# Freeing the key tile from VectorE's drain, and cutting wq into 32, 16 and 16 KB rows

## The chip, the cores and the metric

The kernel runs on one core of one Trainium2 chip. The metric is the device time of one execution in microseconds (us). The engines are named as in the profile: PE is TensorE, PEld its weight loads, DVE is VectorE, ACT is ScalarE, POOL is GpSimd, SP is SyncE; a "q" behind a name (SPq, ACTq, PEq) is that engine's instruction queue. L162 is line 162 of the kernel.

## What is computed

One decode step of a parallel block. `x` has 512 numbers, there are 32 query heads on 8 key heads, and each key head has a cache of 65,536 positions of 128 numbers for the keys and as many for the values, all fp32:

```
xn = layernorm(x)
q = (xn @ wq) as 32 heads of 128
o = softmax(q k^T / sqrt(128)) v          # 4 query heads share a key head
y = x + o @ wo + relu(xn @ w1) @ w2
```

The two caches are 537 MB of the 561 MB that the kernel reads from HBM.

## The kernel before

**Tiles.** `kt` and `vt` hold one chunk each of keys and values: 128 partitions x 16,384 fp32, so 64 KB a row and 8.39 MB (megabytes of 10^6 bytes) a chunk. There are 32 chunks of each (8 heads x 4 parts). Both tiles are single: a new chunk of keys can only be loaded when PE has read the old one. `wt` holds w1 and later w2. `kt` is also used for wq ahead of the first keys, and for wo behind the last.

**SP's queue** issues nearly all loads, in a fixed order: three pieces of wq (L151, L159), w1 (L160), then a wait for the semaphore `kfree` and the first keys K0 (L162). Then a loop: wait for `vfree`, load a chunk of values (L165), wait for `kfree`, load the next keys (L167). Behind it come wo (L173), w2 (L177) and the store (L179). ACT's queue issues two small loads of `x` at the start (L234: 128 rows of 16 bytes into `xT`; L235).

**The start.** ACT, PE, DVE and POOL compute the layer norm of `xT`; POOL then waits for the semaphore `ends` (a piece of wq, L213) and copies xn into `qpad` (L214). PE's "turn" 0 multiplies qpad with wq in `kt`; a turn is 8 rounds of 4 matrix products, each round covering 2,048 columns. Turns 1 to 32 are the scores of the 32 chunks, and turn 33 is wo; all run the same lines (L307 to L320). `turn_scores` is DVE's side: it waits for two rounds each time (`p2d`), transposes 1,024 columns out of PSUM (L367), and gives PE a pair of banks back (`free`). In turn 0, two drains (L369) also hold `free` back until a later piece of wq has landed, so that PE doesn't read columns that aren't there: rounds 4 and 5 need `free` to reach 3, rounds 6 and 7 need 4. In turn 0 a DVE nop (L366) gives `kfree` when PE's rounds are done.

**A chunk.** After the four transposes DVE drains (L384), takes the maximum (L385), exchanges it over PE, and updates the running maximum (L386 to L392). ACT waits for that (`bias`), computes the correction `corr` (L254, which gives `kfree`), then the probabilities (L256, which give `v`). PE waits for the values and the probabilities and multiplies them (L292); behind that L299 gives `vfree`.

Of the kernel before, what the change touches and what calls it, by code (L numbers as in the profile page):

```python
# [8 lines left out]
AF = mybir.ActivationFunctionType  # L9
# [3 lines left out]
P = 128  # L13
# [4 lines left out]
GROUP = 4  # L18
# [19 lines left out]
XA = D // P  # L38
WIDE = 4
ROUNDS = 8  # L40
WQ_CUTS = [4096, 4096, 8192]
WQ_SEMS = ["ends", "k", "wq2"]
WO_CUTS = [16, 8, 8]
W2_CUTS = [6, 4, 2, 1, 1]
W2_SUM = 12
# [4 lines left out]
def take(e, sem, n=1):  # L50

    return e.sem_inc(sem, -n).wait_op(sem, n, "sem-ge")  # L52


def starts(cuts):
    return [sum(cuts[:i]) for i in range(len(cuts) + 1)]
# [3 lines left out]
def attention_and_mlp_kernel(  # L60
# [12 lines left out]
    sp, pe, dve, act, pool = nc.sync, nc.tensor, nc.vector, nc.scalar, nc.gpsimd  # L73
    scale = float(DH) ** -0.5

    def sbuf(name, *shape):
        return nc.alloc_sbuf_tensor(name, list(shape), F32).ap()
# [3 lines left out]
    def sem(name):  # L81
        if name not in sems:
            sems[name] = nc.alloc_semaphore(name)
        return sems[name]

    def after(ins, name, n=1):

        return ins.wait_op(sem(name), n, "sem-ge")
# [33 lines left out]
    diff = sbuf("diff", P, GROUP)  # L122
    corr = sbuf("corr", P, 2, GROUP)
# [18 lines left out]
    v_row = v[0].rearrange("(n p b) d -> n p (b d)", p=P, b=NB)  # L142
    wq_at, wo_at, w2_at = starts(WQ_CUTS), starts(WO_CUTS), starts(W2_CUTS)

# [5 lines left out]

    load = sp.dma_start(kt[:, : WQ_CUTS[0]], wq_row[:, : WQ_CUTS[0]]).then_inc(sem(WQ_SEMS[0]), 16)  # L151
    tc.no_tile_sem_insts.add(load.ins.name)
# [3 lines left out]
    inside = section.enter_context(tc.tile_critical(sync_engine=mybir.EngineType.Pool, no_gpsimd_drain=True))  # L156
    for i in range(1, len(WQ_CUTS)):
        cut = slice(wq_at[i], wq_at[i + 1])
        sp.dma_start(kt[:, cut], wq_row[:, cut]).then_inc(sem(WQ_SEMS[i]), 16)  # L159
    sp.dma_start(wt, w1_row).then_inc(sem("w1"), 16)  # L160
# [23 lines left out]
    def link(ins):  # L184

        if chain[0]:
            after(ins, "pool", chain[0])
        chain[0] += 1
        return ins.then_inc(sem("pool"), 1)
# [21 lines left out]
    link(pool.tensor_mul(st[:, 7:8], st[:, 5:6], st[:, 6:7]))  # L211
    link(pool.tensor_scalar_mul(xn, xc, st[:, 7:8]))
    take(pool, sem("ends"), 16)  # L213
    after(pool.tensor_copy(qpad[:, :XA], xn), "pool", chain[0]).then_inc(sem("q"), 1)  # L214
    f = DFF_ALL
    w1_of = [wt[:, a * f : (a + 1) * f] for a in range(XA)]
# [34 lines left out]
    act.preload_act_table(AF.Exp)  # L251
    with act.Fori(0, NCH):
        take(act, sem("bias"))
        act.activation(corr, diff.unsqueeze(1).to_broadcast([P, 2, GROUP]), AF.Exp).then_inc(sem("kfree"), 1)  # L254
        for g in range(GROUP):
            last = act.activation(  # L256
                probs[:, :, g], tr[:, :, g], AF.Exp, bias=nb_new[:, g : g + 1], scale=scale,
                accum_out=part_sum[:, g : g + 1],
            )
        last.then_inc(sem("v"), 1)  # L260
# [101 lines left out]
    def turn_scores(gates=(), free=None):  # L362

        for s in range(ROUNDS // 2):
            if free and s == ROUNDS // 2 - 1:
                after(dve.nop(), "p2d", s + 1).then_inc(sem(free), 1)  # L366
            ins = after(dve.transpose(tr2[:, s * 1024 : (s + 1) * 1024], pair[s % 2]), "p2d", s + 1)  # L367
            if s < len(gates):
                ins = after(dve.drain(), gates[s], 16)  # L369
            ins.then_inc(sem("free"), 1)  # L370
# [1 line left out]
    dve.memset(ones, 1.0)  # L372
    dve.memset(banks, 0.0).then_inc(sem("zero"), 1)
    after(dve.reciprocal(st[:, 5:6], st[:, 4:5]), "ln", 3).then_inc(sem("ln"), 1)
    turn_scores(["wq2", "wq2"], free="kfree")
    dve.drain()
    dve.tensor_reduce(qall, of_own_row(NQ, XA), axis=AX.X, op=ALU.add).then_inc(sem("dve"), 1)
    take(dve, sem("p2d"), 4)
# [1 line left out]
    with dve.Fori(0, HEADS) as h:  # L380
        dve.tensor_copy(qpad[:, :GROUP], qall[:, bass.ds(h * GROUP, GROUP)]).then_inc(sem("q"), PARTS)
        with dve.Fori(0, PARTS):
            turn_scores()
            dve.drain()  # L384
            dve.reduce_max(m, tr.rearrange("p b i -> p i b")[:, :GROUP, :], axis=AX.X).then_inc(sem("d2p"), 1)  # L385
            after(dve.reduce_max(mg, pma[:GROUP, :P], axis=AX.X), "p2d", 5).then_inc(sem("dve"), 1)  # L386
            after(
                dve.tensor_scalar(dg, ident[:GROUP, :GROUP], mg, -scale, op0=ALU.mult, op1=ALU.mult), "dve", 1  # L388
            ).then_inc(sem("d2p"), 1)
            after(dve.tensor_tensor(nb_new, pmb[:, :GROUP], nb_run, op=ALU.min), "p2d", 6).then_inc(sem("dve"), 1)  # L390
            after(dve.tensor_sub(diff, nb_new, nb_run), "dve", 2).then_inc(sem("dve"), 1)
            after(dve.tensor_copy(nb_run, nb_new), "dve", 3).then_inc(sem("bias"), 1)  # L392
            after(dve.tensor_copy(o_sb.rearrange("p b d -> p (b d)"), acc), "p2d", 7).then_inc(sem("d2p"), 1)  # L393
            dve.tensor_mul(lo_run, lo_run, corr).then_inc(sem("dve"), 1)
            take(dve, sem("p2d"), 8)
            after(dve.tensor_add(lo_run, lo_run, lo_new), "dve", 4).then_inc(sem("dve"), 1)  # L396
            take(dve, sem("dve"), 5)
        dve.reciprocal(diff, lo_run[:, 0, :]).then_inc(sem("dve"), 1)
        dve.memset(nb_run, 3.0e38)
        after(  # L400
            dve.tensor_mul(oT[:, bass.ds(h * GROUP, GROUP)], lo_run[:, 1, :], diff), "dve"
        ).then_inc(sem("dve"), 1)
        take(dve, sem("dve"), 2)
# [53 lines left out]
```

## Time and profile before

| | us |
|---|---|
| median of 3 runs | 1303.04 |
| lowest and highest of them | 1302.91, 1303.61 |
| the profiled execution's own time | 1303.17 |
| its span, first to last instruction | 1301.4 |

So 1.8 us of the profiled execution lie outside the span. The profiled execution shows PE busy 59% of the span, PEld 18%, DVE 21%, ACT 6%, POOL 3%. Starts are counted from the span's start. A landing is the time from a transfer's issue until its semaphore is complete; idle times in brackets stand before an instruction, with what ended them.

### The profile page before, as it was taken

Reading aid. Unit: us, or ns where it says so; the run is one execution under the profiler, and the core shown is the slowest. Engines: PE = TensorE matmul, PEld = TensorE weight load, DVE = VectorE, ACT = ScalarE, POOL = GpSimd, SP = SyncE. Lnnn points to the kernel's source line nnn. Section 1 sums busy time; section 2 is a strip of 40 time slices with the busy share of each in tenths; the row PEclk is TensorE's granted clock in tenths of the full one; section 3 lists DMA queues with packets and bytes.
Section 4 is the critical chain, followed back from the end, with each engine's and each line's share of the span. In section 5 each row is a group of like instructions: output and inputs, shape, how many; then the busy total and the mean of one; then the engine's idle time right before and its main releaser. Section 6 shows DMA issues by size and latency. Waiting matters only on the chain.

```text
span 1301.4 us, 13055 instructions
## 1 busy us (share of the span) xinstructions
PE 771.8 (59%) x5474; PEld 230.8 (18%) x5474; DVE 274.8 (21%) x466; ACT 76.9 (6%) x299; POOL 34.8 (3%) x30
## 2 busy tenths in 40 slices
PE   3365666565665655575566566466566556656667
PEld 1111111111111111121111121111111111112112
DVE  2211222210222221122221122221122221122222
ACT  1000000000000000000000000000000000000000
POOL 1900000000000000000000000000000000000000
PEclk9667877777777777777777787777787776678678
DMA  9999999999999999999999999999999999999998
GB/s 403 451 419 451 419 445 425 441 429 421 449 419 451 419 451 419 443 427 425 445 419 451 419 451 419 445 425 439 431 423 447 419 451 419 447 423 445 425 424 366
DMA packets 11236, 561.02 MB, mean 431 GB/s; under 512 B 1505, under 2 KB 1505, under 8 KB 1890
## 3 DMA queue, kind: packets, MB, share of 16 engines
q1 hardware_dynamic: 11088, 561.00, 99.7%
q10 hardware_dynamic: 146, 0.00, 0.0%
q8 instruction: 1, 0.02, 0.0%
q14 instruction: 1, 0.01, 0.0%
HBM read 560.99 MB, written 0.00 MB: 431 GB/s over the span
## 4 chain that ended last, share of the span: by engine, by line
issue 94%; DMA 3%; POOL 2%; SPq 0%; PE 0%; DVE 0%; POOLq 0%
DMA wt<-w 3%; POOL wt L219 1%; POOL wt L222 0%; POOL wt L224 0%; POOL wt L223 0%; SPq L177 0%; SPq L159 0%; PE banks L345 0%; DVE ysb L418 0%; SPq L151 0%; POOL hT L226 0%; SPq L453 0%; POOLq L156 0%
## 5 line engine op out<-in xcount | busy, mean ns | idle before, releaser
L313 PE MATMUL banks<-kt,qpad 128*32 128x512 f32 x2176 | 311.1, 735 | 308.6 <-PEq L52 306.9
L292 PE MATMUL banks<-vt,probs 128*16 128x512 f32 x2048 | 270.4, 688 | 87.5 <-PEq L52 87.5
L367 DVE STREAM_TRANSPOSE tr<-banks 128x1024 f32<-128x1024 f32 x136 | 170.0, 1250 | 469.9 <-PE banks L313 466.1
L313 PEld LDWEIGHTS banks<-kt,qpad 128*32 128x32 f32 x2176 | 84.4, 132 | 508.2 <-issue 496.2
L292 PEld LDWEIGHTS banks<-vt,probs 128*16 128x16 f32 x2048 | 68.8, 107 | 302.4 <-issue 302.4
L281 PE MATMUL banks<-wt,ones 128*1 128x448 f32 x768 | 118.8, 771 | 0.0
L393 DVE COPY o_sb<-banks 128x512 f32<-128x512 f32 x32 | 22.1, 692 | 457.2 <-PE banks L292 457.2
L254 ACT ACTIVATE corr<-diff 128x8 f32<-128x8 f32 x32 | 6.7, 209 | 1180.1 <-ACTq L52 1180.1
L256 ACT ACTIVATE probs<-tr,nb_new 128x128 f32<-128x128 f32 x128 | 65.9, 522 | 0.0
L276 PE MATMUL banks<-ident,m 128*4 128x128 f32 x32 | 9.8, 306 | 78.9 <-DVE m L385 78.9
L302 PE MATMUL banks<-sel,o_sb 128*128 128x4 f32 x256 | 32.8, 252 | 18.7 <-PEq L52 18.7
L302 PEld LDWEIGHTS banks<-sel,o_sb 128*128 128x128 f32 x256 | 31.0, 191 | 20.6 <-issue 20.6
L226 POOL TENSOR_SCALAR hT<-ysum 128x14 f32<-128x14 f32 x1 | 0.3, 256 | 1218.6 <-DVE ysum L405 1218.6
L385 DVE TENSOR_REDUCE m<-tr 128x4 f32<-128x512 f32 x32 | 32.2, 1005 | 2.9
L281 PEld LDWEIGHTS banks<-wt,ones 128*1 128x1 f32 x768 | 20.1, 99 | 56.5 <-issue 55.9
L277 PE MATMUL banks<-dg,ones 4*128 4x4 f32 x64 | 14.8, 299 | 20.0 <-DVE dg L388 20.0
L256 ACT ACTIVATION_READ_ACCUMULATOR probs<-tr,nb_new 128x1 f32 x128 | 23.9, 187 | 0.0
L276 PEld LDWEIGHTS banks<-ident,m 128*4 128x4 f32 x32 | 2.6, 81 | 108.0 <-DVE m L385 108.0
L219 POOL TENSOR_SCALAR wt<-wt,xn 128x1792 f32<-128x1792 f32 x4 | 19.1, 4797 | 16.4 <-DMA wt<-w 16.4
L277 PEld LDWEIGHTS banks<-dg,ones 4*128 4x128 f32 x64 | 12.0, 233 | 27.2 <-DVE dg L388 27.2
L299 PEld LDWEIGHTS banks<-part_sum,ones 128*128 128x128 f32 x64 | 9.5, 188 | 27.2 <-issue 27.2
L396 DVE TENSOR_TENSOR lo_run<-lo_run,banks 128x8 f32<-128x8 f32 x32 | 5.2, 163 | 40.0 <-DVEq L52 40.0
(69 smaller groups left out, 91.1 us busy)
## 6 DMA issues: line engine op xcount, KB each, us to landing
kt<-wq SPq DMA_DIRECT2D x2, 2048.0 KB, 9.5
kt<-wq SPq DMA_DIRECT2D x1, 4096.0 KB, 21.0
kt<-wo SPq DMA_DIRECT2D x1, 4096.0 KB, 14.5
kt<-wo SPq DMA_DIRECT2D x2, 2048.0 KB, 21.2
wt<-w SPq DMA_DIRECT2D x1, 3584.0 KB, 29.0
wt<-w SPq DMA_DIRECT2D x1, 1536.0 KB, 11.7
wt<-w SPq DMA_DIRECT2D x1, 1024.0 KB, 13.8
kt<-k SPq DMA_DIRECT2D x32, 24.6
```

The lines of the kernel that those rows point to most:

```text
L219: last = pool.tensor_scalar_mul(w1_of[a], w1_of[a], xn[:, a : a + 1])
L256: last = act.activation(probs[:, :, g], tr[:, :, g], AF.Exp, bias=nb_new[:, g : g + 1], scale=scale, accum_out=part_sum[:, g : g + 1],)
L276: after(pe.transpose(pma[:GROUP, :P], m, ident), "d2p").then_inc(sem("p2d"), 1)
L277: after(pe.matmul(pmb[:, :GROUP], ones[:GROUP, :], dg, start=True, stop=True), "d2p", 2).then_inc(sem("p2d"), 1)
L281: ins = pe.matmul(hrow[32 * c : 32 * c + 1, :], ones[:, :1], hb[:, :, 32 * c : 32 * c + 32], start=True, stop=True,)
L292: last = pe.matmul(acc[c : c + WIDE * GROUP, :], probs[:, b : b + WIDE, :].rearrange("p b g -> p (b g)"), vt[:, b * DH : (b + WIDE) * DH], ...
L299: pe.matmul(lo_new[:, 0, :], ones, part_sum, start=True, stop=True).then_inc(sem("vfree"), 1)
L302: last = pe.matmul(lo_new[:, 1, :], o_sb[:, b, :], sel[:, b, :], start=(b == 0), stop=(b == WIDE - 1),)
L313: last = pe.matmul(pair[s // 2 % 2][32 * c : 32 * c + 32, s % 2 * 512 : s % 2 * 512 + 512], qpad, kb[:, s * 16 : s * 16 + 16, c, :], start ...
L367: ins = after(dve.transpose(tr2[:, s * 1024 : (s + 1) * 1024], pair[s % 2]), "p2d", s + 1)
L385: dve.reduce_max(m, tr.rearrange("p b i -> p i b")[:, :GROUP, :], axis=AX.X).then_inc(sem("d2p"), 1)
L393: after(dve.tensor_copy(o_sb.rearrange("p b d -> p (b d)"), acc), "p2d", 7).then_inc(sem("d2p"), 1)
```

## The change

Two things are edited. The pieces of wq are 8,192, 4,096 and 4,096 columns (rows of 32, 16 and 16 KB), not 4,096, 4,096 and 8,192. The first piece signals `ends`, the second a semaphore `wq1` of its own, the third `wq2`. POOL, which waits for `ends`, raises `k` for PE's turn 0 (the second piece did that before), and DVE's two drains of turn 0 wait for `wq1` and `wq2`, not both for `wq2`. And in each chunk `kfree` comes from DVE's drain behind the four transposes (L384), not from ACT's `corr` (L254).

```diff
-WQ_CUTS = [4096, 4096, 8192]
-WQ_SEMS = ["ends", "k", "wq2"]
+WQ_CUTS = [8192, 4096, 4096]
+WQ_SEMS = ["ends", "wq1", "wq2"]
...
     take(pool, sem("ends"), 16)
+    pool.sem_inc(sem("k"), 16)
     after(pool.tensor_copy(qpad[:, :XA], xn), "pool", chain[0]).then_inc(sem("q"), 1)
...
-        act.activation(corr, diff.unsqueeze(1).to_broadcast([P, 2, GROUP]), AF.Exp).then_inc(sem("kfree"), 1)
+        act.activation(corr, diff.unsqueeze(1).to_broadcast([P, 2, GROUP]), AF.Exp)
...
-    turn_scores(["wq2", "wq2"], free="kfree")
+    turn_scores(["wq1", "wq2"], free="kfree")
...
             turn_scores()
-            dve.drain()
+            dve.drain().then_inc(sem("kfree"), 1)
```

## Rows read from the trace of the kernel before

**Rows 1.** The page: DMA busy tenths in 40 slices, SP's queue, HBM traffic.

```profile
DMA  9999999999999999999999999999999999999998
q1 hardware_dynamic: 11088, 561.00, 99.7%
HBM read 560.99 MB, written 0.00 MB: 431 GB/s over the span
```

**Rows 2.** Windows: first to last key wait in the loop; engines, PEclk, DMA share, GB/s.

```profile
64.38:1265.12 1200.74, 723.84 (x5115) 216.40 (x5111) 249.30 (x431) 69.85 (x280) 0.00 (x0) 0.75 1.00 433
```

**Rows 3.** Timeline of PE: start, length, what; score and value products after their loads.

```profile
50.95 8.51 PE L313 MATMUL banks<-kt,qpad 128*32 128x512 f32 x64 [24.48 <-PEq L52]
...
495.86 9.61 PE L292 MATMUL banks<-vt,probs 128*16 128x512 f32 x64 [4.19 <-PEq L52]
515.21 8.49 PE L313 MATMUL banks<-kt,qpad 128*32 128x512 f32 x64 [7.81 <-PEq L52]
534.56 8.76 PE L292 MATMUL banks<-vt,probs 128*16 128x512 f32 x64 [3.44 <-PEq L52]
...
1250.65 9.40 PE L313 MATMUL banks<-kt,qpad 128*32 128x512 f32 x64 [8.59 <-PEq L52]
```

**Rows 4.** Timeline of one chunk, from its last transpose, and of a later chunk.

```profile
485.63 1.25 DVE L367 STREAM_TRANSPOSE tr<-banks 128x1024 f32<-128x1024 f32 x1 [0.47 <-PE banks L313]
...
490.03 0.21 ACT L254 ACTIVATE corr<-diff 128x8 f32<-128x8 f32 x1 [35.53 <-ACTq L52]
...
490.47 0.33 SPq L167 DMA_DIRECT2D kt<-k  x1
...
506.03 0.33 SPq L165 DMA_DIRECT2D vt<-v  x1
...
1227.03 0.33 SPq L167 DMA_DIRECT2D kt<-k  x1
...
1231.29 8.83 PE L292 MATMUL banks<-vt,probs 128*16 128x512 f32 x64 [0.84 <-PEq L52]
```

**Rows 5.** Timeline of the end: wo is issued, the last values' product starts.

```profile
1265.12 1.29 SPq L173 DMA_DIRECT2D kt<-wo  x3
...
1270.01 7.06 PE L292 MATMUL banks<-vt,probs 128*16 128x512 f32 x64 [1.32 <-PEq L52]
```

**Rows 6.** Timeline of the start.

```profile
0.73 0.39 SPq L151 DMA_DIRECT2D kt<-wq  x1
0.97 0.39 ACTq L234 DMA_DIRECT2D xT<-x  x1
...
1.34 0.83 SPq L159 DMA_DIRECT2D kt<-wq  x2
2.22 0.64 SPq L160 DMA_DIRECT2D wt<-w  x1
...
9.48 0.20 ACT L240 ACTIVATE xc<-xT 128x4 f32<-128x4 f32 x1 [6.23 <-DMA xT<-x]
...
15.21 5.88 PE L313 MATMUL banks<-kt,qpad 128*32 128x512 f32 x32 [3.03 <-PEq L52]
...
22.83 3.64 PE L313 MATMUL banks<-kt,qpad 128*32 128x512 f32 x32 [1.75 <-DVEq L369]
...
26.66 0.33 SPq L162 DMA_DIRECT2D kt<-k  x1
```

**Rows 7.** DMA issues of the start, one stretch each, then the store: KB, us to landing.

```profile
kt<-wq SPq DMA_DIRECT2D x1, 2048.0 KB, 7.4
xT<-x ACTq DMA_DIRECT2D x1, 2.0 KB, 8.4
kt<-wq SPq DMA_DIRECT2D x1, 2048.0 KB, 11.7
wt<-w SPq DMA_DIRECT2D x1, 3584.0 KB, 29.0
kt<-k SPq DMA_DIRECT2D x1, 23.9
y<-ysb SPq DMA_DIRECT2D x1, 2.0 KB, 1.4
```

## The prediction, made before the changed kernel ran

> **What bounds the kernel now.** I read the page first, to see which engine is full. None is, but the transfers are: every slice of the DMA line is full, and SP's one queue keeps the 16 DMA engines 99.7% busy for 561 MB [rows 1]. The next question is whether the queue ever runs dry between two chunks, because that is where an earlier release of the keys' tile could pay. The view of windows says no: over the 1200.74 us from the first wait for keys to the last one the DMA share is 1.00 at 433 GB/s [rows 2]. A share is an average, so I went to the timeline of PE and took the starts of the products that wait for a load. Values at 495.86, keys at 515.21, values at 534.56: steps of 19.35 us for 8.39 MB, which is 433 GB/s [rows 3]. From keys K0 (50.95) to keys K31 (1250.65) there are 62 steps in 1199.70 us, which is 19.350 each [rows 3]. The mean over 62 equals the single step to 0.01 us, so all dry spells together are at most 62 x 0.01 = 0.6 us. The kernel is one unbroken stream of rows, with a lead-in ahead of it and a tail behind it. Nothing can win but a shorter stream, lead-in or tail, and anything can lose that leaves the queue empty for a moment.
>
> **Part 1: `kfree` from DVE's drain.** In the chunk shown the last transpose ends at 485.63 + 1.25 = 486.88. `corr` starts at 490.03 and ends at 490.24; SP issues the next keys at 490.47, so 0.23 us behind it [rows 4]. After the change SP should issue at about 486.9 + 0.2 = 487.1, some 3.4 us earlier, in 32 chunks. The naive gain is 32 x 3.4 = 109 us. I cost it at nothing, because the transfer of the values covers it: the values that were issued before those keys land at 495.86, 5.4 us after the issue at 490.47 [rows 3, 4]; the shortest such cover I found among the 32 chunks is 1231.29 - 1227.03 = 4.3 us [rows 4]. An issued load needs far less than that to be ready: the 2 KB store from the otherwise idle queue lands 1.4 us after its issue [rows 7]. So the keys' rows already stand in the queue when the values' last rows go, and standing there 3.4 us longer moves nothing. Without that cover the price would be its lack, chunk by chunk. The next issue behind the keys on SP is that of the next values (506.03 in the row, waiting for `vfree`); it doesn't move, because the values' product that frees `vt` still starts when the values land, and it has 515.21 - 506.03 = 9.2 us of cover [rows 3, 4]. wo is released by the same drain: it is issued at 1265.12 now, 4.9 us ahead of the landing of the last values, and will be about 3 us earlier, with the same result [rows 5].
>
> The drain stands on DVE anyway and now also raises a semaphore; ACT's `corr` no longer does. The trace has no drain with a semaphore by itself. Below, its cost is nothing; above, I take 0.2 us, the whole hand-over that was just seen from `corr` to SP, ahead of the maximum in each chunk. 0.2 us late probabilities would delay PE only where the values had landed already; PE still sits idle 0.84 us for the values in the chunk at 1231.29 and several us in others [rows 3, 4]. So nothing, at both ends.
>
> [...]
>
> **Part 2: the pieces of wq.** Bytes, number of transfers and number of rows are the same (three pieces of 128 rows), so the stream is not shorter. What moves is who waits for what in the first 31 us.
>
> *The gates.* Now PE starts turn 0 at 15.21, stops after 5.88 us, is idle 1.75 us until DVE's drain has seen the last piece, and runs 3.64 us more; SP issues K0 0.19 us behind it, at 26.66 [rows 6]. The new gates let PE run on with the third quarter of wq, so up to 1.75 us of that stall goes. It would only bring K0's issue forward, and that is covered: w1, issued at 2.22, lands at 2.22 + 29.0 = 31.2, 4.6 us later, and K0's landing at 26.66 + 23.9 = 50.6 is one step of 19.35 behind that [rows 6, 7]. So: no gain.
>
> *The long rows.* This is what I think is less obvious. `xT`, 2 KB in 128 tiny rows on ACT's queue, lands 8.4 us after its issue, while the store of the same size and shape lands after 1.4 us [rows 7]. So about 7 us of it is waiting among wq's rows on the same 16 engines. The first piece lands at 0.73 + 7.4 = 8.1, the second at 1.34 + 11.7 = 13.0: 4.9 us for 2 MB, in eight 16 KB rows on each engine, so 0.61 us a row [rows 6, 7]. `xT` lands at 0.97 + 8.4 = 9.4, 1.24 us behind the first piece, which is two rows: it got through as the tenth row of each engine passed. If it goes by rows, ten rows after the change are the eight 32 KB rows of the new first piece, which lands where the old first two did, at 13.0, and two 16 KB rows: 13.0 + 1.2 = 14.3. So `xT` comes 4.9 us later. The bounds are no delay (if it didn't go by rows) and 7.0 us (if the whole wait doubled with the row). I take 4.9, since the wait ends two rows behind a piece.
>
> The layer norm and turn 0 hang on `xT`: 15.21 - 9.48 = 5.7 us from ACT's first instruction to PE's start [rows 6]. The new gate of POOL on `ends` isn't later than that (13.0 against a layer norm that ends near 20). So PE starts turn 0 at 15.21 + 4.9 = 20.1. The last piece lands where it did (just ahead of 22.83), so the drains don't hold PE: the first comes behind two of eight rounds, a quarter of the turn's 9.5 us, and a transpose of 1.25 us [rows 4], at 23.7 or later. So turn 0 takes 5.88 + 3.64 = 9.52 us (score turns took 8.49 to 9.40 [rows 3]), and K0 is issued at 20.1 + 9.5 + 0.2 = 29.8, or at 28.8 with the shortest turn. That is 3.1 us later than now.
>
> *The cover of K0.* The queue's last rows before K0 are w1's, which land at 31.2. K0 must be issued ahead of that by what an issue takes besides its own rows: 1.4 us by the store, 7.4 - 4.9 = 2.5 us by the first piece of wq [rows 7]. So the latest harmless issue lies between 28.8 and 29.9. Against 29.8 the queue is dry for 0 to 1.0 us; I take the middle, 0.45 us. V0 is issued right behind K0 and has 19 us of cover. A dry spell here is not given back, since the stream behind it has no slack.
>
> [...]
>
> **The sum.** Against the profiled execution: 1303.17 + 0 (32 earlier issues) + 0 (gates) + 0.45 (start) = 1303.6. The runs' median is 0.13 below the profiled execution, so 1303.5 for a median. A measurement of this kernel tells apart about 0.2%, 2.6 us; the forecast is no change by that measure.
>
> **The rivals.** *The rows don't matter* (12%): `xT` waits for something else than rows in number, K0 is issued at about 24.9, and the change does nothing: 1303.0. For it: no row shows the order of single rows. Against it: 8.4 us against 1.4. *The wait doubles* (5%), the rival on the slower side: `xT` comes 7.0 us later, PE starts at 22.2, K0 is issued at 31.9, the queue is dry for 2.0 to 3.1 us, and the time is 1305.0 to 1306.1. It decides from a K0 issue at about 31.4 to 32.5 (the latest harmless one plus 2.6 us). Against it: only the first piece's rows get longer, the rows behind it stay at 16 KB. *Hidden gaps* (3%): the 3.4 us in each chunk do buy something, because keys that stand in the queue earlier let each engine run through more evenly; even 0.07 us a step would be 4.5 us, 1298.6. Against it: 62 steps that equal one another. The forecast, a start that costs 0 to 1.0 us, has the remaining 80%.
>
> **Range and chances.** Forecast and first rival span 1303.0 to 1304.0 on the median's scale; with the runs' own spread (-0.1 to +0.6) and about half of the way to the doubled wait, 1302.3 to 1305.0. Faster than 1300.4 needs the hidden gaps: 3%. Slower than 1305.6 needs the upper half of the doubled wait, or a late K0 for another reason: 5%. The same: 92%.
>
> **What would show it.** Right: SP's keys issue some 0.2 us behind the fourth transpose's end, with steps still at 19.35 us; `xT` landing about 13.3 us after its issue; PE's turn 0 starting near 20 with no idle time in its middle; K0 issued near 29.8; K0's scores starting at 51.0 to 52.0, not 50.95. Wrong: a step shorter than 19.3 us, an `xT` that lands at 9.4, or scores of K0 later than 53.

## The result

The changed kernel takes 1305.14 us (median of 22 runs, 1304.13 to 1306.69), the kernel before 1303.26 us (22 runs, 1302.84 to 1304.18). The ratio is 1.0015, with a 95% interval of 1.0009 to 1.0021: 1.9 us slower, too little for the 0.2% that the prediction took as measurable, yet clear of zero. The forecast was 1303.5 us in a range of 1302.3 to 1305.0; the measured median lies 0.14 us above the upper end of that range. The profiled execution took 1305.65 us, with a span of 1303.9 us.

In the changed kernel the lines behind L213 have numbers that are one higher. The page still shows one full stream of loads (compare [rows 1]):

```profile
DMA  9999999999999999999999999999999999999998
q1 hardware_dynamic: 11088, 561.00, 99.6%
```

In the loop, from the first wait for keys to the last one, the view of windows shows the same rate as in [rows 2]:

```profile
63.83:1262.88 1199.05, 723.03 (x5115) 216.32 (x5115) 249.06 (x431) 69.14 (x279) 0.00 (x0) 0.75 1.00 433
```

The timeline of one chunk (it answers to [rows 3, 4]) has the last transpose, the next keys' issue, `corr`, and the two products that wait for a load. (The rows count two records for each matrix product, so x64 is the whole of a turn's 32.)

```profile
487.02 1.25 DVE L368 STREAM_TRANSPOSE tr<-banks 128x1024 f32<-128x1024 f32 x1 [0.47 <-PE banks L314]
...
488.55 0.33 SPq L167 DMA_DIRECT2D kt<-k  x1
...
491.46 0.21 ACT L255 ACTIVATE corr<-diff 128x8 f32<-128x8 f32 x1 [35.84 <-ACTq L52]
...
497.88 8.76 PE L293 MATMUL banks<-vt,probs 128*16 128x512 f32 x64 [3.36 <-PEq L52]
...
517.23 9.55 PE L314 MATMUL banks<-kt,qpad 128*32 128x512 f32 x64 [8.67 <-PEq L52]
```

SP issues the keys 0.28 us behind the last transpose (488.27) and 2.9 us ahead of `corr`; under the old release it would have been 0.23 us behind `corr`'s end, at 491.9, so the release came 3.35 us earlier. The step from values to keys is 19.35 us, as before. All that gain is hidden.

The start is where the two traces part (it answers to [rows 6, 7]). First the timeline, then the issues with their us to landing:

```profile
13.56 0.20 ACT L241 ACTIVATE xc<-xT 128x4 f32<-128x4 f32 x1 [10.31 <-DMA xT<-x]
...
19.29 9.34 PE L314 MATMUL banks<-kt,qpad 128*32 128x512 f32 x64 [3.02 <-PEq L52]
...
28.83 0.33 SPq L162 DMA_DIRECT2D kt<-k  x1
...
52.35 9.88 PE L314 MATMUL banks<-kt,qpad 128*32 128x512 f32 x64 [23.71 <-PEq L52]
```

```profile
xT<-x ACTq DMA_DIRECT2D x1, 2.0 KB, 12.5
wt<-w SPq DMA_DIRECT2D x1, 3584.0 KB, 28.9
kt<-k SPq DMA_DIRECT2D x1, 23.1
```

`xT` lands 12.5 us after its issue, not 8.4; everything behind it moves by 4.08 us (13.56 against 9.48 on ACT, 19.29 against 15.21 on PE). Turn 0 runs without its stall, K0 is issued at 28.83 instead of 26.66, and its scores start 1.40 us late (52.35 against 50.95). K0 lands at 28.83 + 23.1 = 51.9, while w1, the load ahead of it, landed at 2.22 + 28.9 = 31.1: 20.8 us, where a step is 19.35. So K0 landed 1.4 to 1.5 us too late.

A load raises its semaphore 16 times and has landed with the last of them; the traces of both kernels have the 16 times of each piece of wq and of each chunk. In the kernel before, K0's sixteen come from 50.12 to 50.61 us, the middle one at 50.26; here they come from 50.44 to 51.91, the middle one at 50.95. So K0 isn't late as one piece: its first part comes 0.3 us later than there, the middle 0.7, the last 1.3. The parts don't catch up with one another: those of the next keys, K1, come from 89.12 to 90.69 (before: 88.82 to 89.31).

In this profile two more pieces came on top. The last values' product starts at 1272.03, which is 2.02 us behind 1270.01 [rows 5], so 0.6 us more were lost in loads behind K0 (V1 to K4, by their landings, though they were issued 7.9 to 11.9 us ahead of the landing of the load before them); and that product took 9.31 us, not 7.06:

```profile
1272.03 9.31 PE L293 MATMUL banks<-vt,probs 128*16 128x512 f32 x64 [3.36 <-PEq L52]
...
1301.27 0.34 SPq L179 DMA_DIRECT2D y<-ysb  x1
```

The windows over that product give PE's granted clock (the column behind POOL): 1.00 in the kernel before, and a mean of 0.75 in the changed one. PE had been idle 1.32 us ahead of the product in the one [rows 5], 3.36 us in the other.

```profile
1270.01:1277.10 7.09, 7.09 (x65) 2.05 (x65) 0.00 (x0) 0.00 (x0) 0.00 (x0) 1.00 1.00 430
```

```profile
1272.03:1281.30 9.27, 9.27 (x65) 2.19 (x65) 0.00 (x0) 0.00 (x0) 0.00 (x0) 0.75 0.98 421
```

Behind it the slowed products of PE, not the last load of w2, ended the chain. The views of the chain that ended last show it, the kernel before first:

```profile
1283.19 14.95 DMA wt<-w
```

```profile
1285.04 9.68 PE banks L314 x64
```

From the start of the last values' product to the end of the span it is 1303.9 - 1272.03 = 31.9 us, against 1301.4 - 1270.01 = 31.4 us. Only 0.16 us of these 0.5 lie ahead of the store's issue (1301.27 - 1272.03 = 29.24, against 29.08); the rest lies behind it.

### The profile page after: what moved, and what is told of

Same layout as the page of the kernel before. It is cut to its first block, busy times and chain, and to the rows that moved or that the text cites. A ratio compares the mean times of both kernels' runs of the same rounds, so it can differ in the third digit from the quotient of the medians.

```text
span 1303.9 us, 13056 instructions
## 1 busy us (share of the span) xinstructions
PE 772.9 (59%) x5474; PEld 231.1 (18%) x5474; DVE 274.7 (21%) x466; ACT 76.0 (6%) x299; POOL 34.8 (3%) x30
## 5 line engine op out<-in xcount | busy, mean ns | idle before, releaser
L293 PE MATMUL banks<-vt,probs 128*16 128x512 f32 x2048 | 267.2, 681 | 81.3 <-PEq L52 81.3
L282 PE MATMUL banks<-wt,ones 128*1 128x448 f32 x768 | 122.2, 791 | 0.0
## 6 DMA issues: line engine op xcount, KB each, us to landing
wt<-w SPq DMA_DIRECT2D x1, 3584.0 KB, 28.9
```

Of the source, the lines that this page charges most:

```text
L282: ins = pe.matmul(hrow[32 * c : 32 * c + 1, :], ones[:, :1], hb[:, :, 32 * c : 32 * c + 32], start=True, stop=True,)
L293: last = pe.matmul(acc[c : c + WIDE * GROUP, :], probs[:, b : b + WIDE, :].rearrange("p b g -> p (b g)"), vt[:, b * DH : (b + WIDE) * DH], ...
```

## The experiments

The theory from here on is A: all is lost at the start, because K0 is issued too late behind w1. The rivals: the earlier release in each chunk disturbs the stream (B), or the long rows cost something of their own (C).

**Each part alone.** The pieces of wq alone, which is the changed kernel with ACT's release as before:

```diff
-        act.activation(corr, ..., AF.Exp)
+        act.activation(corr, ..., AF.Exp).then_inc(sem("kfree"), 1)
...
-            dve.drain().then_inc(sem("kfree"), 1)
+            dve.drain()
```

> The new pieces of wq alone; ACT gives the keys' tile free as before. Theory A (the start: 32 KB rows hold xT back, K0 is issued too late behind w1): all of the loss is here, K0 issued near 28.8 us, its scores near 52.3 instead of 50.95, time 1304.7 to 1305.4. Theory B (the earlier release in each chunk disturbs the stream): no loss here beyond 0.4 us, 1303.0 to 1303.7.

Measured: 1305.63 us against 1303.06 (ratio 1.0024, 1.0013 to 1.0035; its runs spread from 1303.54 to 1313.02). The timeline of its start:

```profile
28.90 0.33 SPq L162 DMA_DIRECT2D kt<-k  x1
...
52.26 8.29 PE L314 MATMUL banks<-kt,qpad 128*32 128x512 f32 x48 [23.54 <-PEq L52]
```

The release by the drain alone, in the kernel before:

```diff
-        act.activation(corr, ..., AF.Exp).then_inc(sem("kfree"), 1)
+        act.activation(corr, ..., AF.Exp)
...
-            dve.drain()
+            dve.drain().then_inc(sem("kfree"), 1)
```

> The release of the keys' tile by the drain alone; wq in 16, 16 and 32 KB rows as before. Theory A: K0 issued at 26.7, its scores at 50.95, the next keys issued 3.4 us earlier in each chunk, steps of 19.35 us, time within 0.4 us of the kernel before (1303.3). Theory B: slower by 0.5 to 1.9 us, with steps longer than 19.35 us in the first chunks.

Measured: 1303.05 us against 1303.06 (ratio 0.9999, 0.9990 to 1.0008). K0 and its scores:

```profile
26.46 0.33 SPq L162 DMA_DIRECT2D kt<-k  x1
...
50.74 8.50 PE L313 MATMUL banks<-kt,qpad 128*32 128x512 f32 x64 [24.48 <-PEq L52]
```

B falls: 32 releases, each over 3 us earlier (3.35 to 3.66 us in the changed kernel's trace), cost nothing and gain nothing. The loss belongs to the pieces of wq. (The ratios in this document compare the means of the runs, so the few long ones above pull at them.)

**Take the long rows away.** The changed kernel with wq in four pieces of 16 KB rows:

```diff
-WQ_CUTS = [8192, 4096, 4096]
-WQ_SEMS = ["ends", "wq1", "wq2"]
+WQ_CUTS = [4096, 4096, 4096, 4096]
+WQ_SEMS = ["ends", "k", "wq1", "wq2"]
...
-    pool.sem_inc(sem("k"), 16)
```

> The changed kernel, but wq in four pieces of 16 KB rows (the gates in their new order, the drain's release kept). Theory A: xT lands at 9.4 us, PE starts turn 0 at 15.2, K0 is issued near 24.9, and the loss is gone: within 0.4 us of the kernel before (1303.3). Theory B: still 0.5 to 1.9 us slower. If the gates' order itself costs something, it shows here too.

Measured: 1304.67 us against 1303.06 (ratio 1.0012, 1.0003 to 1.0021). By its time this speaks against A. The trace tells two things apart. The start is healed, and so is every load up to the last values (1270.03 against 1270.01). Turn 0 starts at 15.13 and K0 is out 1.6 us earlier than in the kernel before, which gains nothing, as its scores start at 50.98:

```profile
15.13 6.87 PE L313 MATMUL banks<-kt,qpad 128*32 128x512 f32 x48 [3.03 <-PEq L52]
...
25.05 0.33 SPq L162 DMA_DIRECT2D kt<-k  x1
...
50.98 9.43 PE L313 MATMUL banks<-kt,qpad 128*32 128x512 f32 x64 [26.11 <-PEq L52]
```

But the store, issued at 1299.13 (before: 1299.09), lands 3.1 us later instead of 1.4 [rows 7]:

```profile
y<-ysb SPq DMA_DIRECT2D x1, 2.0 KB, 3.1
```

So the 1.6 us of this kernel are at its very end, where the changed kernel's store landed after 1.5 us. The same kernel was loaded and measured once more:

> The kernel with four pieces of 16 KB once more, loaded anew. In its first profile all loads land as in the kernel before, yet it is 1.6 us slower, because the store's 16 completions came 3.1 us after its issue instead of 1.4. If that was a matter of where the program or its output lay in that load, it is gone: 1303.0 to 1303.5. If it belongs to the kernel, 1304.5 to 1305 again.

1304.59 us against 1303.21 (ratio 1.0009, 1.0000 to 1.0018), with the store landing after 3.0 us and the loads on time: it belongs to the kernel. It has one load more than the kernel before and the changed one, hence this test, the kernel before with 2 KB loaded for nothing:

```diff
     sp.dma_start(wt, w1_row).then_inc(sem("w1"), 16)
+    sp.dma_start(spare, x.rearrange("(p a) -> p a", p=P)).then_inc(sem("spare"), 16)
```

> The kernel before with one more load, 2 KB that nobody uses, behind w1. If one load more is what makes the store's completions late (1.6 us in the kernel with four pieces and in the one with a quarter of V0 ahead, which both have one load more): the store lands 3.1 us after its issue and the time is 1304.5 to 1305. If not: 1303.0 to 1303.5.

1305.28 us against 1303.24 (ratio 1.0016, 1.0007 to 1.0025). Its loads are 0.3 to 0.5 us late, and the store:

```profile
y<-ysb SPq DMA_DIRECT2D x1, 2.0 KB, 2.8
```

One load more costs some 1.4 to 1.7 us at the store, in all three kernels here that have it (the third is the one with a quarter of V0 ahead, below), and in none of those with the old number. Why, these runs don't show. For the changed kernel, which has the old number, it plays no part.

**Leave the long rows, but get xT through.** The changed kernel, with `xT` issued by SP ahead of wq:

```diff
+    first = sp.dma_start(xT, x.rearrange("(p a) -> p a", p=P)).then_inc(sem("x"), 16)
     load = sp.dma_start(kt[:, : WQ_CUTS[0]], ...)
...
-    act.dma_start(xT, x.rearrange("(p a) -> p a", p=P)).then_inc(sem("x"), 16)
```

> The changed kernel with its 32 KB rows, but SP issues xT ahead of wq in its own queue. Theory A: xT lands within 3 us, wq starts 0.6 us later because its issue stands behind, K0 is issued near 25 (set by the last piece of wq), and no dry spell: 1303.3 to 1303.9, slower than before by at most those 0.6 us. Theory B: 1303.8 to 1305.8.

Measured: 1304.09 us against 1303.06 (ratio 1.0007, 0.9998 to 1.0016), undecided by its interval. `xT` landed 1.8 us after its issue, and the timeline shows K0 issued as early as in the kernel before, though not near 25 as I expected:

```profile
1.18 0.42 SPq L154 DMA_DIRECT2D kt<-wq  x1
...
26.62 0.33 SPq L165 DMA_DIRECT2D kt<-k  x1
...
51.52 8.74 PE L316 MATMUL banks<-kt,qpad 128*32 128x512 f32 x64 [25.07 <-PEq L52]
```

Its scores are 0.57 us late, and 0.45 us of that is wq's own issue, at 1.18 instead of 0.73. w1 lands at 2.67 + 29.1 = 31.8, K0 at 26.62 + 24.5 = 51.1, one step of 19.35 later, so no time is lost between them. The other half of the 1.0 us in the median isn't in its profile. So this run is consistent with A and doesn't prove it.

**Delay K0 and change nothing else.** In the kernel before, 1, 2 or 4 transposes of 1.25 us on DVE stand ahead of the release of K0 (into `vt`, which is still empty):

```diff
-                after(dve.nop(), "p2d", s + 1).then_inc(sem(free), 1)
+                after(dve.nop(), "p2d", s + 1)
+                for i in range(2):
+                    late = dve.transpose(vt[:, i * 1024 : (i + 1) * 1024], pair[1])
+                late.then_inc(sem(free), 1)
```

> The kernel before, with one extra transpose of 1.25 us on DVE (into the still empty vt) ahead of the release of K0 in turn 0, so that K0 is issued near 28.0 instead of 26.66. Theory A (a load that is issued late behind w1 costs 3.75 us besides its rows, as K0 did in the changed kernel, so it must be out by 27.5): 0.5 us slower, 1303.8. The prediction's own sizes (harmless up to 28.8 to 29.9): no loss, 1303.3.

> The same with two extra transposes: K0 near 29.3. Theory A with 3.75 us: 1.8 us slower, 1305.1. The prediction's sizes: 0 to 0.5 us slower, 1303.3 to 1303.8.

> The same with four extra transposes: K0 near 32.0, when the queue is empty. Theory A with 3.75 us: 4.5 us slower, 1307.8. The prediction's sizes: 2.1 to 3.2 us slower, 1305.4 to 1306.5.

Measured against 1303.64 us: 1303.61 (ratio 1.0000, 0.9991 to 1.0009), 1304.76 (1.0016, 1.0007 to 1.0025) and 1305.85 us (1.0018, 1.0009 to 1.0027). The timelines of K0's issue and scores, with one, two and four transposes; behind them, in the same order, K0's lines among the issues with the us to landing:

```profile
27.86 0.33 SPq L162 DMA_DIRECT2D kt<-k  x1
...
51.50 9.01 PE L313 MATMUL banks<-kt,qpad 128*32 128x512 f32 x60 [25.06 <-PEq L52]
```

```profile
28.92 0.33 SPq L162 DMA_DIRECT2D kt<-k  x1
...
51.56 8.97 PE L313 MATMUL banks<-kt,qpad 128*32 128x512 f32 x56 [25.19 <-PEq L52]
```

```profile
31.10 0.33 SPq L162 DMA_DIRECT2D kt<-k  x1
...
53.21 7.37 PE L313 MATMUL banks<-kt,qpad 128*32 128x512 f32 x52 [26.92 <-PEq L52]
```

```profile
kt<-k SPq DMA_DIRECT2D x1, 23.2
```

```profile
kt<-k SPq DMA_DIRECT2D x1, 22.3
```

```profile
kt<-k SPq DMA_DIRECT2D x1, 21.8
```

The second has K0 at the same time as the changed kernel (28.92 against 28.83), with wq and `xT` as before. Its ratio is about the same, 1.0016 against 1.0015, but three of its 11 runs, at 1307.6 to 1307.8 us, make that; its median moved by 1.1 us, that of the changed kernel by 1.9. So a late K0 alone is enough for a loss, and by the medians for more than half of this one. Theory A's own size is not borne out: K0's 23.1 - 19.35 = 3.75 us besides its rows in the changed kernel, taken as a fixed need of any late issue, asked for 0.5, 1.8 and 4.5 us and got 0.0, 1.1 and 2.2.

**The changed kernel once more**, loaded anew:

> The changed kernel once more, loaded anew, for a second profile. If the start's loss belongs to it, K0's scores start 1.3 to 1.5 us later than in the kernel before again; whether the further 0.6 us that its first profile lost in the loads of V1 to K4 and the 0.5 us at the end come back is open.

1304.92 us against 1303.21 (ratio 1.0011, 1.0002 to 1.0020). Its profile:

```profile
28.83 0.33 SPq L162 DMA_DIRECT2D kt<-k  x1
...
52.03 8.35 PE L314 MATMUL banks<-kt,qpad 128*32 128x512 f32 x64 [23.39 <-PEq L52]
...
1270.90 7.06 PE L293 MATMUL banks<-vt,probs 128*16 128x512 f32 x64 [1.34 <-PEq L52]
```

K0's scores are 1.08 us late again; the last values are 0.89 us late, so nothing was lost in between, and the last product ran in 7.06 us. So the two further pieces of the first profile come and go. This profiled execution took 1303.95 us, the second fastest of its 11 runs; what the median run lost beyond it, 1.0 us, stands in no profile.

**Give K0 cover.** The changed kernel with part of V0 issued ahead of the wait for K0, so that the queue lasts longer. First a quarter of V0:

```diff
+    sp.dma_start(vt[:, :V0], v_row[0][:, :V0]).then_inc(sem("v0"), 16)    # V0 = 4096
     take(sp, sem("kfree"))
     sp.dma_start(kt, k[0, 0]).then_inc(sem("k"), 16)
+    take(sp, sem("vfree"))
+    sp.dma_start(vt[:, V0:], v_row[0][:, V0:]).then_inc(sem("v"), 16)
...
+    act.wait_ge(sem("v0"), 16)
     with act.Fori(0, NCH):
```

> The changed kernel with its 32 KB rows and its late xT, but SP issues the first quarter of V0 (4,096 columns, 2.1 MB) behind w1 and ahead of the wait for K0; the rest of V0 follows K0. Theory A (the whole loss of the stream is K0 being issued too late behind w1): K0 is still issued near 28.8 but has some 4.8 us more cover, so the values V1 and all later loads land as in the kernel before, and the time is within 0.4 us of it, but for what the end adds (up to 0.5 us, as in the changed kernel's profile). Rival C (the longer rows or their late xT cost something else): 1.4 to 2 us slower, as the changed kernel.

1305.83 us against 1303.21 (ratio 1.0015, 1.0006 to 1.0024): a miss, for two reasons that its trace shows. It has one load more, and its store lands after 3.1 us. And K0, which lands 4.9 us later behind a quarter of V0 (28.18 + 27.3 = 55.5 against 50.6), now makes K1 late: K1 is issued at 66.43, 3.5 us ahead of the landing of V0's rest (28.62 + 41.3 = 69.9), lands 24.2 us later, and its scores start 1.34 us late (89.44 before). The timeline, then K1's line among the issues:

```profile
66.43 0.33 SPq L168 DMA_DIRECT2D kt<-k  x1
...
90.78 2.79 PE L321 MATMUL banks<-kt,qpad 128*32 128x512 f32 x12 [9.88 <-PEq L53]
```

```profile
kt<-k SPq DMA_DIRECT2D x1, 24.2
```

So an eighth, and wq in two pieces to keep the number of loads:

```diff
-WQ_CUTS = [8192, 4096, 4096]
-WQ_SEMS = ["ends", "wq1", "wq2"]
+WQ_CUTS = [8192, 8192]
+WQ_SEMS = ["ends", "wq2"]
...
-    turn_scores(["wq1", "wq2"], free="kfree")
+    turn_scores(["wq2", "wq2"], free="kfree")
...
-V0 = 4096
+V0 = 2048
```

> The changed kernel with its 32 KB first piece and its late xT, but with cover for K0: the first 2,048 columns of V0 (1.05 MB, 2.4 us) are issued behind w1, ahead of the wait for K0. wq comes in two pieces of 32 KB rows, so that the number of loads stays the same. Theory A (an issue has to lead the end of the queue by some 4 us; K0's 2.35 us in the changed kernel and K1's 3.5 us with a quarter of V0 ahead were too short): K0 leads by 4.8 us or more, K1 by 5 to 6, all values and keys from V0 on land as in the kernel before to 0.1 us, although xT is as late as in the changed kernel; time 1303.0 to 1303.6 if the store completes in 1.4 us. Rival C (the long rows or the late xT cost something by themselves): loads 1 to 1.4 us late.

1303.30 us against 1303.24 (ratio 1.0000, 0.9991 to 1.0009). `xT` and K0 are even later than in the changed kernel, K0 landed 23.0 us after its issue, one step behind the eighth of V0 (2.22 + 31.6 = 33.8), and from K1 on all loads stand 0.13 to 0.16 us behind those of the kernel before:

```profile
14.41 0.20 ACT L247 ACTIVATE xc<-xT 128x4 f32<-128x4 f32 x1 [11.16 <-DMA xT<-x]
...
30.13 0.33 SPq L164 DMA_DIRECT2D kt<-k  x1
...
53.60 8.44 PE L321 MATMUL banks<-kt,qpad 128*32 128x512 f32 x64 [23.66 <-PEq L53]
...
89.60 9.21 PE L321 MATMUL banks<-kt,qpad 128*32 128x512 f32 x64 [10.39 <-PEq L53]
```

Among the issues, the eighth of V0 and K0:

```profile
vt<-v SPq DMA_DIRECT2D x1, 1024.0 KB, 31.6
kt<-k SPq DMA_DIRECT2D x1, 23.0
```

With the long rows, the late `xT` and the early release all in place, cover for K0 gives back the whole loss. That settles A against C: the rows and the late `xT` cost nothing by themselves once K0 has cover. No kernel here beats the kernel before; this one, the release alone and the one with a single transpose equal it.

## Why the prediction was wrong

**What bounds the kernel, part 1 and the gates: right.** The steps stayed at 19.35 us, the keys' issue moved 3.35 us (3.4 forecast) and bought nothing, and the release alone measures 0.9999. No run shows the 0.07 us a step by which the rival of the hidden gaps was sized: with the release alone the 62 steps from K0's scores to K31's take 1199.69 us (50.74 to 1250.43), so 19.35 each. The stall in turn 0 went and gained nothing (with 16 KB rows K0 was even out 1.6 us earlier, and its scores started at 50.98).

**The long rows: the mechanism right, the size off.** `xT` goes by rows, and the packets in the trace say so: its 16-byte rows start in groups of 16, in the changed kernel from 4.75, 5.98, 7.20, 8.41, 9.63, 10.84 and 12.06 us, one group per 32 KB row; with the 16 KB rows of the kernel before the groups lie 0.61 us apart. The eighth group goes 0.01 us behind the seventh, and the 4-byte packets with which this queue's load ends start 0.61 us behind it, at 12.68, so `xT` waited for one 16 KB row behind the first piece, not two: it came 4.08 us later, 4.9 forecast. Turn 0 took 9.34 us, not 9.5. So K0 was issued at 28.83, not 29.8. It was out a microsecond earlier than I feared, and still did more harm: this error hid part of the next one.

**The cover of K0: this is the step that failed.** I took what an issue needs besides its own rows from loads into an empty queue, 1.4 to 2.5 us. With K0 at 28.83 these bounds give a loss of at most 28.83 + 2.5 - 31.2 = 0.1 us. Measured were 1.1 to 1.5 us, and K0's scores started at 52.35 and 52.03, beyond the 51.0 to 52.0 that I had named. The runs allow a table: the lead is how far ahead of the landing of the load in front of it a load was issued; "late" is its landing less that landing less a step of 19.35 (landings are given to 0.1 us).

| load | issued | load ahead lands | lead | late |
|---|---|---|---|---|
| K0, kernel before | 26.66 | 31.2 | 4.6 | 0.0 |
| K0, an eighth of V0 ahead | 30.13 | 33.8 | 3.7 | 0.0 |
| K1, a quarter of V0 ahead | 66.43 | 69.9 | 3.5 | 1.4 |
| K0, one transpose | 27.86 | 31.2 | 3.4 | 0.5 |
| K0, changed kernel | 28.83 | 31.1 | 2.3 | 1.5 |
| K0, changed, loaded anew | 28.83 | 31.2 | 2.4 | 1.1 |
| K0, pieces alone | 28.90 | 31.1 | 2.2 | 1.3 |
| K0, two transposes | 28.92 | 31.1 | 2.2 | 0.7 |
| K0, four transposes | 31.10 | 31.0 | -0.1 | 2.5 |

In this table a lead of 3.7 us or more lost nothing and one of 2.2 to 3.5 us lost 0.5 to 1.5 us, one profile to a row, so the border between them is not sharp: with the pieces alone K1 was issued some 3.8 us ahead (an estimate: V0 landed at 29.62 + 41.5 = 71.1, and PE's second product for the maximum, which starts 1.55 us ahead of K1's issue in the kernel before, started at 65.62 and took 0.2 us longer), yet its scores started at 90.85, 0.2 us more than a step behind V0's product at 71.30. With the queue already empty the loss is 2.5 us, the old upper bound; what I had not thought of is that a load issued into the last rows of another loses more than the lack of lead explains. At a lead of 2.3 us and a need of 2.5 us it should lose 0.2 us and lost 0.7 to 1.5.

The sixteen parts show where the difference lies. In the changed kernel w1's middle part came at 30.98, so a need of 2.5 us gives K0's middle part 28.83 + 2.5 - 30.98 = 0.35 us of loss; it lost 0.6, and the last part 1.4 (1.5 in the table, by its coarser landings). So the need was some 0.3 us too small, and the spread of the parts, for which the prediction had no term, made the landing 0.8 us later still. Why the parts differ is open.

**The sum.** The start's term was 0.45 us; it measured 1.1 to 1.5. The median moved by 1.9 and, loaded anew, by 1.7. The rest came in one profile as 0.6 us in the loads behind K0 and 0.5 us at the end, and not in the other profile. The end has a pattern of its own in all 14 profiles: where PE was idle 1.0 to 1.3 us ahead of the last values' product, that product took 7.06 us and the store was issued as far behind its start as in the kernel before (to 0.03 us); where PE was idle 3.4 to 4.3 us, it took 8.8 to 9.8 us, and the store came 0.0 to 0.9 us later. Kernels whose K0 was on time have it too (9.17 us with four pieces of wq, 9.42 us with an eighth of V0 ahead), so it isn't tied to a late K0. The loss as a whole goes with K0's lateness in the last experiment; how the 0.4 to 0.8 us beyond K0's own landing come about stays open. The rival on the slower side, the doubled wait of `xT`, had the right amount for the wrong reason.

## What to carry to other kernels

A queue that never runs dry hid 32 earlier releases here (1303.05 us against 1303.06), but it also made one late issue permanent (K0's scores 1.08 us late, the last values 0.89, in the second profile of the changed kernel): check the lead of each load over the end of the one ahead of it, the first one of a loop above all, and keep what the trace shows to be harmless (4.1 us and more in the loop of the kernel before) rather than a latency read from an empty queue (1.4 to 2.5 us). The tiny rows of `xT` waited on another queue for long rows, one by one (it landed 12.5 us after its issue, not 8.4), so longer rows in a first load can delay a chain that this load itself doesn't hold up. And where a time moves by a thousandth, look at each landing: an experiment that healed the start looked like a failure because its store landed after 3.1 us instead of 1.4.

## What was not expected of the hardware

A load of the same bytes, issued 2.2 to 3.5 us ahead of the end of the queue, landed 0.5 to 1.5 us late, and 0.0 us late with 3.7 us; into an empty queue it was 2.5 us late. The lateness differs between the sixteen parts of a load (0.3 to 1.3 us in the changed kernel's K0), and the delay stays with the stream to its end (the last values 2.02 and 0.89 us late in the changed kernel's two profiles). And one load more in the program, even 2 KB that nobody reads, came with a final store that landed 2.8 to 3.1 us after its issue instead of 1.4 to 1.6, in four profiles of three kernels; the cause is open.
